# Handing over each MLP group's result one to three steps later, with one pool of four PSUM banks, in an attention and gated-MLP kernel

## The chip, the cores and the metric

The kernel runs on one core of one Trainium2 chip. The metric is device time in microseconds (us), lower is better. A core has five engines that run their own instruction streams in order and wait for each other on semaphores: TensorE (PE, with its weight loads shown as PEld), VectorE (DVE), ScalarE (ACT), GpSimd (POOL) and SyncE (SP), which here only issues DMA transfers. TensorE writes its products to PSUM, which has eight banks; each tile of this kernel's PSUM pools is one bank of 128 x 512 fp32.

## The reference, cut to what matters

Eight batches, eight heads, 576 positions, head width 64. Attention is masked by blocks of 64; its output, with the heads side by side (576 x 512), goes into a gated MLP whose gate mixes positions.

```python
scores = scale * np.matmul(q, k.transpose(0, 1, 3, 2))
scores = np.where(mask, scores, -1000000000.0)
attn = np.exp(scores - np.max(scores, axis=-1, keepdims=True))
attn = attn / (np.sum(attn, axis=-1, keepdims=True) + 1e-09)
x = np.matmul(attn, v)
...
h = np.maximum(x @ w_in, 0.0)
u, v = (h[..., :d_ff // 2], h[..., d_ff // 2:])
v_n = (v - mu) / np.sqrt(var + 1e-06)
v_s = np.einsum('ts,bsd->btd', w_spatial, v_n) + b_spatial[None, :, None]
out = (u * v_s) @ w_out
```

## The kernel before, in words

Operands are held as a high part and a remainder, so that most products are three matmuls: high by high, high by low, low by high. The work is cut into *steps*. A pair of heads of one batch takes NS = 7 steps, one for each slot of `SLOTS`: slots 0 and 1 are query tiles 0 and 1 of the two heads, 2 and 3 are query tile 2, 4 and 5 are query tile 3, and slot 6 is the last 64 queries of both heads. A batch has four pairs, so 28 steps.

For a pair (b, pr), by tile names in the profile:

- Scores `s`. `scores` (L261) issues slots 0 to 3 in step 0 and slots 4 and 5 in step 2, `scores_last` (L280) slot 6 as two banks in step 5. The two heads of a slot pair use different rows of the array, and the code issues their matmuls in turn. The banks come from `ps_s`, four of them.
- `exps` (L293) on DVE adds the mask and finds the maximum (L309, L318), which frees the score bank; ACT takes the exponential into tile `p` (L325).
- `norm` (L331): two small DVE instructions on the sums, then POOL scales `p` (L343).
- `transposes` (L384): DVE turns `p` into `q` in 32 x 32 blocks (L395, L400), and `move` issues 16 DMA transfers on SP that bring the blocks of `q` to their places in the single tile `turned` (L410). For batch 0 and the very last pair `transposes_pe` does it on TensorE instead.
- `av` (L431): the products of `turned` with `v` in two banks, `avl` and `avh` (L445, L462). `x_evac` (L423) takes the high part out on ACT and the remainder on DVE, into tile `x` (L426, L427).
- `prep_pair` (L222) splits the next pair's `raw` keys and queries into `hi` (ACT) and `lo` (DVE for the first 512 query columns, POOL for the rest, L232).

The MLP of batch b (`moe`, L477) is 29 *groups*, each one PSUM bank: five `mv` groups (gate half, positions in rows, with mean and variance taken over the row afterwards), eight `mu` groups (the other half), and then for each half z of the positions four `ms` groups (the mixing over positions) and four `mo` groups (output). A group's matmuls are followed at once, in the program's text, by all the work on its result: the `mv` group by evacuation (L499), statistics, normalization and splitting into `vh` and `vl` (L515 to L552); `mu` by L567; `ms` by the product with `u` on DVE (L592), the high part `gh` on ACT (L593) and the remainder `gl` on POOL, or on DVE for the fourth; `mo` by a copy on ACT (L612) and a DMA from ACT's queue. These groups are taken from a queue in the step loop at a little over one per step, beside the attention of the next batch. Their banks come from `ps_m`, two of them; transposes on TensorE and `av` have `ps_t`, two more.

The step loop (L677 to L735) sets the order in which the program is written. The instructions are then put in their final order, engine by engine, by a list scheduler that keeps to the written order as a priority and places an instruction earlier where its inputs and its tile's buffer are free. Each engine runs its own list in order.

Of the kernel before, what the change touches and what calls it, by code (L numbers as in the profile page):

```python
# [17 lines left out]
P = 128  # L18
# [16 lines left out]
RUN2, LAST, AV_AT, MOVES = 2, 5, 2 * NS + 1, 4  # L35
# [7 lines left out]
def kernel(  # L43
# [32 lines left out]
    ps_t = ctx.enter_context(tc.tile_pool(name="ps_t", bufs=2, space=PSUM))  # L76
    ps_m = ctx.enter_context(tc.tile_pool(name="ps_m", bufs=2, space=PSUM))
# [50 lines left out]
    def prep_w(hi, lo, w, rows, cols, name):  # L128
# [12 lines left out]
        f = ff_p.tile([P, 512], F32, tag="vr", name=f"f{name}", bufs=2)[:, :n]  # L141
# [63 lines left out]

    raws = {}
# [15 lines left out]
    def prep_pair(b, pr):  # L222
# [8 lines left out]
        for n, cs in enumerate((slice(S, Q8), slice(0, HT), slice(HT, S), slice(Q8, KQ))):  # L231
            (nc.vector if n == 0 else nc.gpsimd).tensor_tensor(  # L232
                out=lo[:, cs], in0=raw[:, cs], in1=hi[:, cs].bitcast(F32), op=ALU.subtract
            )
            yield
# [119 lines left out]
    def transposes_pe(b, pr, i):  # L355
# [3 lines left out]
        def bank(tag):  # L359
            return ps_t.tile([P, 512], F32, tag="t", name=f"t_{b}_{pr}_{tag}")  # L360
# [62 lines left out]
    def x_evac(b, pr, av, q0, n):  # L423
        x = x_tiles(b, pr)
        qs = slice(q0, q0 + n)
        nc.scalar.copy(x[:, 0, qs], av[:, :n])  # L426
        nc.vector.tensor_tensor(  # L427
            out=x[:, 1, qs], in0=av[:, :n], in1=x[:, 0, qs].bitcast(F32), op=ALU.subtract
        )

    def av(b, pr):  # L431
# [3 lines left out]
        al = ps_t.tile([P, 512], F32, tag="t", name=f"avl_{b}_{pr}")  # L435
        ah = ps_t.tile([P, 512], F32, tag="t", name=f"avh_{b}_{pr}")
# [22 lines left out]
        for c in range(5):  # L459
# [9 lines left out]
        x = xts[(b, pr)]  # L469

        nc.gpsimd.tensor_scalar(
            out=tails[b][:, pr], in0=x[:, :, FULL * P:].bitcast(F32), scalar1=1.0, scalar2=1.0,
            op0=ALU.mult, op1=ALU.mult,
        )


    def moe(b):  # L477
# [3 lines left out]
        u = ff_p.tile([P, ND, S], F32, tag="u", name=f"u_{b}")  # L481

        def v_group(c):
            ps = ps_m.tile([P, 512], F32, tag="m", name=f"mv_{b}_{c}")
            vr = ff_p.tile([P, DH], F32, tag="vr", name=f"vr_{b}_{c}", bufs=2)
# [3 lines left out]
            if c < FULL:  # L489
# [9 lines left out]
                nc.scalar.activation(vr, ps, AF.Relu)  # L499
            else:  # L500

                m = S - FULL * P
                for k in range(NC):
# [6 lines left out]
                nc.scalar.copy(vr[:m, :], ps[m:2 * m, :])  # L510
                nc.vector.tensor_tensor(out=vr[:m, :], in0=ps[:m, :], in1=vr[:m, :], op=ALU.add)
                nc.vector.tensor_scalar(
                    out=vr[:m, :], in0=vr[:m, :], scalar1=0.0, scalar2=None, op0=ALU.max
                )
            nc.vector.bn_stats(out=st[:m, 0:6], in_=vr[:m, :])  # L515
# [267 lines left out]
```

## Time and profile before

| | |
|---|---|
| runs of the kernel | 790.95, 791.2, 800.11 us; median 791.2 us |
| the profiled execution | 788.31 us, of which the span from first to last instruction is 786.5 us |
| mean granted TensorE clock | 0.961 |
| busy: DVE, ACT, POOL | 485.7, 424.9, 305.6 us |
| DMA | 92.05 MB, mean 117 GB/s |

A profile page has six parts: busy time of each engine; the span in 40 slices; DMA queues; the chain of work that ended last, followed back from the end; the costliest groups of instructions with the idle time of their engine before them; and DMA issues. Matmuls overlap each other, and their ends are modelled, so a busy share of PE is not its share of peak. Where a row of the timeline has a number in brackets, the engine stood idle that long before it, and the name behind the arrow is what ended the idle time. Line numbers are those of the code above.

### The profile page before, as it was taken

To read this page: it belongs to the slowest core of one execution; us is meant where nothing else is said; L and a number is where in the kernel's file an instruction comes from. 1 tells how busy PE (TensorE), PEld (TensorE's weight loads), DVE (VectorE), ACT (ScalarE), POOL (GpSimd) and SP (SyncE) were. 2 spreads that over 40 slices of the span, in tenths; PEclk is the share of its full clock that TensorE was granted. 3 is DMA by queue.
4 is the path that set the end of the run, shared out by engine and by line. 5 is a ranking of instruction groups with operands and counts; after the bars stand their busy time and mean duration, and the time that the engine had idled before them with its cause. 6 is when DMAs were issued, how large, how long until landed. Compare 5 with 4: busy or idle time off the path is not lost.

```text
span 786.5 us, 16421 instructions
## 1 busy us (share of the span) xinstructions
PE 719.0 (91%) x5729; PEld 621.8 (79%) x5729; DVE 485.7 (62%) x1639; ACT 424.9 (54%) x1148; POOL 305.6 (39%) x481
## 2 busy tenths in 40 slices
PE   8989689988999899998989979899798989999998
PEld 5656467877889788887779968798687877899898
DVE  6985797656766566547676465766576656731431
ACT  6876645545645465535664446555464446552542
POOL 4876446435154323334334441443224533231011
PEclk9989989997999999899999999999999999999999
DMA  6633344456345553255442453445613554333001
GB/s 208 197 115 90 105 122 131 105 141 172 88 120 155 157 135 76 74 154 151 130 123 72 134 163 95 131 110 146 185 46 108 155 158 103 82 89 89 1 8 54
DMA packets 42150, 92.05 MB, mean 117 GB/s; under 512 B 9298, under 2 KB 18002, under 8 KB 42068
## 3 DMA queue, kind: packets, MB, share of 16 engines
q1 hardware_dynamic: 32852, 81.56, 38.1%
q10 hardware_dynamic: 9216, 9.44, 3.5%
q8 instruction: 45, 0.74, 0.4%
q14 instruction: 37, 0.30, 0.1%
HBM read 38.18 MB, written 9.44 MB: 61 GB/s over the span
## 4 chain that ended last, share of the span: by engine, by line
PE 34%; DVE 21%; ACT 12%; POOL 7%; DMA 6%; issue 6%; SPq 3%; DVEq 0%; ACTq 0%; POOLq 0%
PE ms L585 12%; PE mo L606 11%; DVE q L395 6%; ACT p L325 4%; DMA raw<-qk 3%; DVE p L309 3%; POOL p L343 3%; POOL lo L232 3%; SPq L410 3%; ACT vr L535 3%; DVE st L515 2%; DVE vl L542 2%; PE s L274 2%; PE avl L445 2%; DMA outT<-o 2%
## 5 line engine op out<-in xcount | busy, mean ns | idle before, releaser
L325 ACT ACTIVATE p<-p,nmax 128x128 f32<-128x128 f32 (+4 forms) x288 | 166.9, 580 | 121.7 <-DVE nmax L309 92.4
L343 POOL TENSOR_SCALAR p<-p,ssum 128x128 f32<-128x128 f32 (+4 forms) x288 | 164.7, 588 | 170.7 <-DVE ssum L339 106.5
L395 DVE STREAM_TRANSPOSE q<-p 128x384 f32<-128x384 f32 (+1 forms) x189 | 113.6, 621 | 56.8 <-POOL p L343 31.9
L562 PE MATMUL mu<-x,wi_hi 128*128 128x288 f32 x512 | 117.9, 306 | 11.8 <-ACT u L567 3.4
L309 DVE CUSTOM_DVE_ANT_0 p<-s,mask 128x128 f32<-128x128 f32 (+3 forms) x256 | 116.0, 473 | 15.0 <-PE t L372 6.8
L232 POOL TENSOR_TENSOR lo<-raw,hi 128x288 fp32r<-128x288 f32 (+1 forms) x84 | 65.2, 798 | 142.1 <-ACT hi L229 142.1
L562 PEld LDWEIGHTS mu<-x,wi_hi 128*128 128x128 f32 x512 | 86.5, 190 | 25.2 <-DVE x L427 7.1
L494 PE MATMUL mv<-wi_hi,x 128*128 128x512 f32 x256 | 88.7, 408 | 0.0
L585 PE MATMUL ms<-ws_hi,vh 128*128 128x288 f32 x256 | 78.7, 307 | 8.1 <-ACT u L567 6.2
L585 PE MATMUL ms<-ws_lo,vh 128*128 128x288 f32 x256 | 77.0, 301 | 0.0
L585 PE MATMUL ms<-ws_hi,vl 128*128 128x288 f32 x256 | 77.0, 301 | 0.0
L592 DVE TENSOR_TENSOR u<-ms,u 128x288 f32<-128x288 f32 x64 | 29.0, 453 | 73.4 <-PE ms L590 73.1
L606 PE MATMUL mo<-gh,wo_hi 128*128 128x288 f32 x256 | 72.3, 304 | 1.1 <-DVE u L592 0.7
L606 PE MATMUL mo<-gh,wo_lo 128*128 128x288 f32 x256 | 71.9, 301 | 0.0
L562 PE MATMUL mu<-x,wi_lo 128*128 128x288 f32 x256 | 71.7, 300 | 0.0
L274 PE MATMUL s<-hi 64*128 64x128 f32 (+2 forms) x224 | 56.1, 384 | 11.2 <-DVE nmax L309 8.5
L594 POOL TENSOR_TENSOR gl<-u,gh 128x288 fp32r<-128x288 f32 x48 | 38.8, 809 | 70.7 <-ACT gh L593 70.1
L593 ACT CAST gh<-u 128x288 fp32r<-128x288 f32 x64 | 27.5, 430 | 71.2 <-DVE u L592 71.2
L585 PEld LDWEIGHTS ms<-ws_hi,vh 128*128 128x128 f32 x256 | 49.7, 194 | 13.8 <-ACT u L567 8.9
L494 PEld LDWEIGHTS mv<-wi_hi,x 128*128 128x128 f32 x256 | 49.1, 192 | 13.7 <-ACT o L612 1.8
L445 PE MATMUL avh<-turned,v 128*64 128x128 f32 x868 | 59.2, 293 | 0.0
L445 PEld LDWEIGHTS avh<-turned,v 128*64 128x64 f32 x868 | 54.7, 149 | 0.0
(122 smaller groups left out, 1600.8 us busy)
## 6 DMA issues: line engine op xcount, KB each, us to landing
turned<-q SPq DMA_DIRECT2D x216, 100.0 KB, 2.2
turned<-q SPq DMA_DIRECT2D x216, 96.0 KB, 2.2
raw<-qk SPq DMA_DIRECT2D x31, 608.0 KB, 4.1
v<-v SPq DMA_DIRECT2D x32, 320.0 KB, 3.3
outT<-o ACTq DMA_DIRECT2D x64, 144.0 KB, 2.0
rwi<-w_in SPq DMA_DIRECT2D x8, 512.0 KB, 4.9
rwo<-w_out SPq DMA_DIRECT2D x4, 512.0 KB, 4.7
rws<-w_spT SPq DMA_DIRECT2D x4, 288.0 KB, 3.4
```

Source lines behind the costliest of these rows:

```text
L232: (nc.vector if n == 0 else nc.gpsimd).tensor_tensor(out=lo[:, cs], in0=raw[:, cs], in1=hi[:, cs].bitcast(F32), op=ALU.subtract)
L274: nc.tensor.matmul(banks[(b, pr, i + hd)][:, o:o + n], a[js, qs], k[js, :n], start=(m == 0), stop=(m == len(parts) - 1),)
L309: nc.vector.tensor_tensor_reduce(out=pt[:, o:o + n], in0=bk[:, o:o + n], in1=mask[:, 512 - n:], scale=-0.125, scalar=BIG, op0=ALU.add, op1 ...
L325: nc.scalar.activation(pt[:, o:o + n], pt[:, o:o + n], AF.Exp, bias=mx, scale=-1.0, accum_out=ssum[:, s0 + r:s0 + r + 1],)
L343: nc.gpsimd.tensor_scalar(out=pt[:, o:o + w], in0=pt[:, o:o + w], scalar1=ssum[:, r:r + 1], scalar2=1.0, op0=ALU.mult, op1=ALU.mult,)
L395: nc.vector.transpose(to[:, :, o:o + 32 * n].rearrange("p r (c j) -> p c r j", j=32), pt[:, :n * P].rearrange("p (c r j) -> p c r j", r=4, ...
L445: nc.tensor.matmul(out[js, (t0 - q0) * P:(t1 + 1 - q0) * P].rearrange("p (t a j) -> p a t j", a=4, j=32), vt[:, c, js], src[:, :, o:o + 32 ...
L494: nc.tensor.matmul(ps, xs[k][:, j, cs], w[:, k, DH:], start=(n == 0), stop=(n == 3 * NC - 1),)
L562: nc.tensor.matmul(ps[:, :HT], w[:, k, ds], xs[k][:, j, zs], start=(n == 0), stop=(n == 3 * NC - 1),)
L585: nc.tensor.matmul(ps[:, :HT], a[:, ds], w[:, k, zs], start=(n == 0), stop=False)
L594: (nc.vector if dc == ND - 1 else nc.gpsimd).tensor_tensor(out=gl[:, dc, :], in0=uz, in1=gh[:, dc, :].bitcast(F32), op=ALU.subtract)
L606: nc.tensor.matmul(ps[:, :HT], w[:, k, es], a[:, k, :], start=(n == 0), stop=(n == 3 * ND - 1),)
```

## The change

Results are handed over later. A small agenda, `later(steps, phase, f)`, holds a piece of code until a step and one of four places in it; `due(phase)` runs what has come due.

```diff
+    def later(steps, phase, f):
+        todo.setdefault((now[0] + steps, phase), []).append(f)
+
+    def due(phase):
+        for f in todo.pop((now[0], phase), ()):
+            f()
```

One pool of four banks takes the place of two pools of two; `transposes_pe` and `av` take their banks from it too.

```diff
-    ps_t = ctx.enter_context(tc.tile_pool(name="ps_t", bufs=2, space=PSUM))
-    ps_m = ctx.enter_context(tc.tile_pool(name="ps_m", bufs=2, space=PSUM))
+    ps_m = ctx.enter_context(tc.tile_pool(name="ps_m", bufs=4, space=PSUM))
...
-        al = ps_t.tile([P, 512], F32, tag="t", name=f"avl_{b}_{pr}")
-        ah = ps_t.tile([P, 512], F32, tag="t", name=f"avh_{b}_{pr}")
+        al = ps_m.tile([P, 512], F32, tag="m", name=f"avl_{b}_{pr}")
+        ah = ps_m.tile([P, 512], F32, tag="m", name=f"avh_{b}_{pr}")
```

The work behind each group becomes closures. For `x` and the four kinds of group:

```diff
+        later(1, 0, hi)
+        later(1, 1, lo)
...
+            later(1, 0, evac)
+            later(1, 2, stats)
+            later(2, 1, scale)
+            later(2, 2, normal)
+            later(3, 1, rest)
...
+            later(0 if dc == ND - 1 else 1, 2 if dc == ND - 1 else 0, gate)
+            later(0 if dc == ND - 1 else 1, 2 if dc == ND - 1 else 1, split_g)
...
+            later(1, 0, leave)
```

An `ms` group now waits in the queue until all five `mv` results are complete, and an `mo` group until its four `gh` and `gl` are; the credit for groups is capped at two; the `mo` group takes its matmuls k by k, the three products of a k together:

```diff
-            for a, ws in ((gh, (wo_hi, wo_lo)), (gl, (wo_hi,))):
-                for k in range(ND):
-                    for w in ws:
+            for k in range(ND):
+                for a, w in ((gh, wo_hi), (gh, wo_lo), (gl, wo_hi)):
...
-        credit += rate
-        while credit >= 1.0 and queue:
-            queue.pop(0)()
+        credit = min(credit + rate, 2.0)
+        while credit >= 1.0 and queue and queue[0][0]():
+            queue.pop(0)[1]()
```

From batch 1 on, slots 0 and 1 are issued in step 0, slots 2 and 3 in step 1; `av` moves from step 15 to step 16 after its pair's start, and a batch's groups enter the queue one step after its last `av`:

```diff
-        if here and i == 0:
-            scores(*here, (0, 1, 2, 3))
...
+        if here:
+            if i == 0:
+                scores(*here, (0, 1, 2, 3) if boot else (0, 1))
+            elif i == 1 and not boot:
+                scores(*here, (2, 3))
+            elif i == 2:
+                scores(*here, (4, 5))
...
-RUN2, LAST, AV_AT, MOVES = 2, 5, 2 * NS + 1, 4
+LAST, AV_AT, BOOT_AV, MOVES = 5, 2 * NS + 2, NS + 2, 4
...
+                    later(1, 3, lambda b=pairs[of][0]: begin(b))
```

Work changes engine: all of `lo` goes to POOL (288 + 288 + 288 + 352 columns for each pair), the fourth `gl` too, and `vs_b`, a copy of 64 x 512 once in a batch, from DVE to ACT.

```diff
-        for n, cs in enumerate((slice(S, Q8), slice(0, HT), slice(HT, S), slice(Q8, KQ))):
-            (nc.vector if n == 0 else nc.gpsimd).tensor_tensor(
+        for cs in (slice(S, S + HT), slice(0, HT), slice(HT, S), slice(S + HT, KQ)):
+            nc.gpsimd.tensor_tensor(
...
-            (nc.vector if dc == ND - 1 else nc.gpsimd).tensor_tensor(
...
+                nc.gpsimd.tensor_tensor(
```

The rows `vr` have three buffers instead of two, and the preparation of the weights in batch 0 and 1 is spread a few steps later.

Three places of the order in which the instructions now stand, with buffer numbers behind the names (`s_6_0_1` is the score bank of batch 6, pair 0, slot 1). First TensorE at the start of pair (6, 0). Before:

```order
L274 MATMUL s_6_0_0_6580<-hi_6_0_6345 128x128
L274 MATMUL s_6_0_1_6581<-hi_6_0_6345 128x128
L274 MATMUL s_6_0_0_6580<-lo_6_0_6346,hi_6_0_6345 128x128
L274 MATMUL s_6_0_1_6581<-lo_6_0_6346,hi_6_0_6345 128x128
L274 MATMUL s_6_0_0_6580<-hi_6_0_6345,lo_6_0_6346 128x128
L274 MATMUL s_6_0_1_6581<-hi_6_0_6345,lo_6_0_6346 128x128
L274 MATMUL s_6_0_0_6580<-hi_6_0_6345 128x256
L274 MATMUL s_6_0_1_6581<-hi_6_0_6345 128x256
```

TensorE at the same place, after:

```order
L297 MATMUL s_5_3_6_1_6479<-hi_5_3_6051,lo_5_3_6052 128x288
L285 MATMUL s_6_0_0_6547<-hi_6_0_6355 128x128
L285 MATMUL s_6_0_0_6547<-lo_6_0_6356,hi_6_0_6355 128x128
L285 MATMUL s_6_0_0_6547<-hi_6_0_6355,lo_6_0_6356 128x128
L285 MATMUL s_6_0_0_6547<-hi_6_0_6355 128x256
L285 MATMUL s_6_0_0_6547<-lo_6_0_6356,hi_6_0_6355 128x256
L285 MATMUL s_6_0_0_6547<-hi_6_0_6355,lo_6_0_6356 128x256
L464 MATMUL avl_5_1_6358<-turned_122,v_5_1_6106 64x4x2x32 x2
L464 MATMUL avl_5_1_6358<-turned_122,v_5_1_6106 64x128 x2
L464 MATMUL avh_5_1_6359<-turned_122,v_5_1_6106 64x128 x14
L481 MATMUL avh_5_1_6359<-turned_122,v_5_1_6106 64x64 x10
L606 MATMUL mu_4_1_3_6392<-x_4_0_4916,wi_hi_110 128x288
```

Slot 0 now stands alone, right behind the previous pair's last scores and ahead of `av`; slot 1 follows five groups later (`mu_4_1_3`, then the four `ms_4_0`). Over the whole program, of the matmuls of slots 0 and 1 from batch 1 on, 61 of 168 with 128 columns and 60 of 168 with 256 stand away from their sibling head before, and 150 and 119 after; of slots 2 to 5, 25 of 336 before and 5 after.

Second TensorE at the head of batch 4's MLP. Before:

```order
L274 MATMUL s_5_2_0_6004<-hi_5_2_5727,lo_5_2_5728 128x256
L445 MATMUL avl_4_3_5736<-turned_125,v_4_3_5503 64x4x2x32 x2
L445 MATMUL avl_4_3_5736<-turned_125,v_4_3_5503 64x128 x2
L445 MATMUL avh_4_3_5737<-turned_125,v_4_3_5503 64x128 x14
L462 MATMUL avh_4_3_5737<-turned_125,v_4_3_5503 64x64 x10
L494 MATMUL mv_4_0_5834<-wi_hi_113,x_4_3_5766 128x512
L494 MATMUL mv_4_0_5834<-wi_lo_114,x_4_3_5766 128x512
```

TensorE at the same place, after:

```order
L285 MATMUL s_5_2_0_5946<-hi_5_2_5735,lo_5_2_5736 128x256
L464 MATMUL avl_4_3_5738<-turned_122,v_4_3_5498 64x4x2x32 x2
L464 MATMUL avl_4_3_5738<-turned_122,v_4_3_5498 64x128 x2
L464 MATMUL avh_4_3_5739<-turned_122,v_4_3_5498 64x128 x14
L481 MATMUL avh_4_3_5739<-turned_122,v_4_3_5498 64x64 x10
L665 MATMUL mo_3_1_1_5772<-gh_3_1_5581,wo_hi_112 128x288
L665 MATMUL mo_3_1_1_5772<-gh_3_1_5581,wo_lo_113 128x288
L665 MATMUL mo_3_1_1_5772<-gl_3_1_5582,wo_hi_112 128x288
```

Before, the product that needs `x_4_3` comes directly behind the `av` that makes it; after, three whole `mo` groups of batch 3 stand between. Between two `av` there now stand 8, 7, 7 and 7 groups in each of the batches 1 to 5; before, counted by their matmuls, 8.6, 8.8, 8.7 and 2.9, the last of these just ahead of the `av` shown. Behind the very last `av` stand 39 groups, where there were 28.

Third DVE around the `ms` groups of the first half of batch 4. Before:

```order
L592 TENSOR_TENSOR u_4_5804<-ms_4_0_0_6392,u_4_5804 128x288
L309 ISA p_5_3_4_6495,nmax_5_3_4_6493<-s_5_3_4_6431,mask_96 128x512
L309 ISA nmax_5_3_4_6493 128x1
L592 TENSOR_TENSOR u_4_5804<-ms_4_0_1_6439,u_4_5804 128x288
L592 TENSOR_TENSOR u_4_5804<-ms_4_0_2_6467,u_4_5804 128x288
L592 TENSOR_TENSOR u_4_5804<-ms_4_0_3_6502,u_4_5804 128x288
L594 TENSOR_TENSOR gl_4_0_6391<-u_4_5804,gh_4_0_6390 128x288
L395 STREAM_TRANSPOSE q_5_3_6485<-p_5_3_0_6321 128x3x4x32
```

DVE, after:

```order
L406 STREAM_TRANSPOSE q_5_3_6439<-p_5_3_4_6445 128x4x4x32
L347 TENSOR_SCALAR ssum_5_3_6_6516<-ssum_5_3_6_6516 128x1
L443 TENSOR_TENSOR x_5_1_6407<-avl_5_1_6358,x_5_1_6407 128x256
L443 TENSOR_TENSOR x_5_1_6407<-avh_5_1_6359,x_5_1_6407 128x320
L350 RECIPROCAL ssum_5_3_6_6516<-ssum_5_3_6_6516 128x1
L406 STREAM_TRANSPOSE q_5_3_6439<-p_5_3_5_6487 128x4x4x32
L639 TENSOR_TENSOR u_4_5909<-ms_4_0_0_6423,u_4_5909 128x288
L406 STREAM_TRANSPOSE q_5_3_6439<-p_5_3_6_6517 128x4x4x32
L411 STREAM_TRANSPOSE q_5_3_6439<-p_5_3_6_6517 128x2x32
L639 TENSOR_TENSOR u_4_5909<-ms_4_0_1_6462,u_4_5909 128x288
```

The products of the `ms` groups have moved behind the previous pair's transposes and behind the two evacuations of `av`; the fourth `gl` has left DVE.

More of the change, by code (lines that the diff above doesn't have):

```diff
@@ L735 @@
                     moving.append(move(b, pr))
-    for q in queue:
-        q()
+        due(3)
 def words(a):
```

249 lines of the change are left out of this document (144 added, 105 removed).

## The prediction

> **What bounds the kernel now.** I read the page first, for the span and the chain of work that ended last, then the windows, cut at the `av` of pair 1 of each batch.
>
> ```profile
> span 786.5 us, 16421 instructions
> ...
> PE 34%; DVE 21%; ACT 12%; POOL 7%; DMA 6%; issue 6%; SPq 3%; DVEq 0%; ACTq 0%; POOLq 0%
> ```
>
> ```profile
> 0.00:67.30 67.30, 57.59 (x392) 37.54 (x392) 50.75 (x171) 48.42 (x134) 44.06 (x65) 0.92 0.50 161
> 67.30:143.20 75.90, 63.81 (x455) 53.31 (x454) 57.41 (x179) 43.91 (x116) 38.47 (x53) 0.93 0.41 112
> 143.20:235.40 92.20, 83.50 (x686) 72.62 (x685) 60.43 (x205) 50.25 (x137) 38.32 (x61) 0.94 0.48 129
> 235.40:329.10 93.70, 88.05 (x701) 77.77 (x702) 58.68 (x204) 50.05 (x137) 35.11 (x58) 0.93 0.45 123
> 329.10:422.60 93.50, 86.56 (x706) 76.03 (x708) 59.08 (x204) 49.89 (x137) 35.52 (x58) 0.96 0.45 124
> 422.60:515.40 92.80, 85.34 (x706) 74.99 (x708) 59.06 (x204) 49.78 (x137) 35.52 (x58) 0.98 0.45 124
> 515.40:607.90 92.50, 85.05 (x707) 74.74 (x708) 58.99 (x204) 50.12 (x137) 35.55 (x58) 0.98 0.46 125
> 607.90:697.90 90.00, 84.54 (x704) 74.89 (x700) 56.46 (x199) 48.82 (x135) 32.83 (x56) 0.98 0.43 114
> 697.90:786.50 88.60, 84.59 (x689) 79.88 (x688) 24.81 (x69) 33.69 (x78) 10.24 (x15) 1.00 0.17 50
> ```
>
> After the window and its length the columns are busy time of PE, PEld, DVE, ACT and POOL, then the granted clock. From 143 us on a batch takes 90 to 94 us, and only PE is near its limit: DVE is busy 59 of 93 us. The chain passes through every engine, so it is no single engine that sets the end but PE plus what it waits for. What a steady batch could give back is PE's idle time plus what the lower clock took (one minus the granted clock, times the window). For the six windows from 143.2 to 697.9 that is 8.7 + 5.5, 5.7 + 6.6, 6.9 + 3.7, 7.5 + 1.9, 7.5 + 1.9 and 5.5 + 1.8, together 63 us. For 67.3 to 143.2 it is 12.1 + 5.3 = 17 us. The last window, with MLP work alone, stands at clock 1.00.
>
> The waits of PE in one steady batch (who waited, for whom, total, times, longest):
>
> ```profile
> PE avl L445 <- DMA turned<-q: 3.1, 1, 3.1
> PE s L274 <- DVE nmax L309: 1.3, 1, 1.3
> PE mu L562 <- DVE x L427: 1.3, 1, 1.3
> PE ms L585 <- ACT u L567: 1.0, 1, 1.0
> ```
>
> Four single waits, each at one place of the order: `av` comes too soon after the last one for the transfers between; slots 0 to 3 ask for four score banks at once; `mu` wants the newest `x`; `ms` wants the bank of a `mu` not yet evacuated. In the window from 67.3 us on the two-bank pool shows the same fault:
>
> ```profile
> PE mv L505 <- ACT vr L499: 4.6, 1, 4.6
> PE mu L562 <- ACT u L567: 2.6, 2, 2.2
> ```
>
> **The change, part by part.** *The wait of `av`.* The transfers of `turned` may start only when the last `av` has read it.
>
> ```profile
> 448.87 11.53 SPq L410 DMA_DIRECT2D turned<-q  x16
> ```
>
> ```profile
> 458.16 0.32 PE L274 MATMUL s<-hi 64*128 64x128 f32 x1
> ...
> 458.84 0.28 PE L274 MATMUL s<-hi,lo 64*128 64x256 f32 x1
> 462.19 0.87 PE L445 MATMUL avl<-turned,v 128*64 128x256 f32 x8 [3.07 <-DMA turned<-q]
> ```
>
> ```profile
> 515.33 0.87 PE L445 MATMUL avl<-turned,v 128*64 128x256 f32 x8
> ...
> 518.24 0.40 PE L606 MATMUL mo<-gh,wo_lo 128*128 128x288 f32 x1
> ...
> 519.37 0.33 PE L274 MATMUL s<-hi 64*128 64x128 f32 x2
> ...
> 520.16 0.34 PE L274 MATMUL s<-hi 64*128 64x384 f32 x2
> ```
>
> ```profile
> 506.55 0.40 PE L585 MATMUL ms<-ws_hi,vh 128*128 128x288 f32 x1 [0.99 <-ACT u L567]
> 506.79 0.30 PE L585 MATMUL ms<-ws_lo,vh 128*128 128x288 f32 x1
> 506.92 0.30 PE L585 MATMUL ms<-ws_hi,vl 128*128 128x288 f32 x1
> ```
>
> Sixteen issues take SP 11.53 us, the last lands 1.8 us later (460.40 to 462.19), and the `av` itself takes 2.9 us (515.33 to 518.24): 16.2 us from `av` to `av` at least. The new order has at least 7 groups between two. Matmuls start 0.13 us apart (506.79, 506.92), so a group of 12 is 1.6 us or more, and 7 groups, the scores (some 4 us, an estimate from the 0.79 us that slots 0 and 1 take together, 519.37 to 520.16) and the `av` are 18 us. The wait of 3.1 us goes, with about 2 us to spare.
>
> *The newest `x`.* Three `mo` groups (4.8 us) now stand behind `av`, and the evacuations fit beside them: the wait of 1.3 us goes. *Four banks.* A group may find its bank occupied only when the fourth group back is not evacuated, 6 us earlier; that covers the waits for `u` and `vr`. Every new late step on ACT or DVE is covered by that distance; without it, one such wait costs the 1.0 us of its row.
>
> *What is late next.* Two of the four banks are held by `avl` and `avh`, so the third group behind an `av` waits for DVE's `x` instruction. Here the durations are from the same steady batch:
>
> ```profile
> L232 POOL TENSOR_TENSOR lo<-raw,hi 128x288 fp32r<-128x288 f32 x8 | 6.7, 864 | 22.1 <-ACT hi L229 22.1
> ```
>
> ```profile
> L395 DVE STREAM_TRANSPOSE q<-p 128x384 f32<-128x384 f32 x16 | 8.4, 555 | 5.1 <-DMA turned<-q 5.1
> L395 DVE STREAM_TRANSPOSE q<-p 128x512 f32<-128x512 f32 x12 | 8.4, 707 | 4.4 <-POOL p L343 4.4
> L309 DVE CUSTOM_DVE_ANT_0 p<-s,mask 128x512 f32<-128x512 f32 x8 | 5.3, 662 | 0.0
> L232 DVE TENSOR_TENSOR lo<-raw,hi 128x512 fp32r<-128x512 f32 x4 | 2.7, 685 | 0.2 <-ACT hi L229 0.2
> ```
>
> Between slots 4 and 5 being ready and the `x` of `avl`, DVE now has four transposes of 0.56, one of 0.71, two maxima of 0.66, four shorter ones (at most 0.66 each) and small sums: 7 to 8 us. PE meanwhile has slot 6 and slot 0 (1.6), `av` (2.9) and two groups (3.2 to 3.5): about 8 us. That is a near tie. I allow 0.6 us of new waiting for each of 27 pairs, 16 us in all; the bounds are 0 (DVE ahead) and 3.6 us a pair (POOL's whole new `lo`, 1,216 columns at 0.864 us for 288, in front of the scaling that a transpose waits for). I stay near the lower end because that scaling is ahead of the last piece in POOL's order.
>
> *Work that changes engine.* POOL's `lo` grows from 704 to 1,216 columns, at 0.864 us for 288 a growth of 1.5 us for each pair, and DVE loses 0.685 us. POOL is busy 36 of 93 us, so this lies beside other work, unless it delays a scaling as just bounded. The fourth `gl` on POOL ends perhaps 0.4 us later than on DVE; in the tail, where no scores stand between, that may show twice: +1 us. The `vs_b` copy and the k-by-k order of `mo` issue the same matmuls and cost nothing that PE sees.
>
> *Scores apart.* Slot 0 alone takes 458.16 to about 459.0, 0.84 us for one head; together the two heads take 519.37 to 520.16, 0.79 us. So a head that stands alone adds about 0.42 us for six matmuls, near 0.06 for one of 128 columns and 0.08 for one of 256. 89 more of the first and 59 more of the second stand alone: +10 us; 20 of the wide ones join again: -2 us. I take +8 us; the bounds are 0 and 12.
>
> *The clock.* The wait of 506.55, one batch earlier:
>
> ```profile
> 412.32 0.61 PE L585 MATMUL ms<-ws_hi,vh 128*128 128x288 f32 x1 [0.99 <-ACT u L567]
> 412.73 0.44 PE L585 MATMUL ms<-ws_lo,vh 128*128 128x288 f32 x1
> ```
>
> The same 0.99 us wait is followed by matmuls of 0.44 us here and of 0.30 us at 506.79, so a short wait may or may not cost clock. [...] By the row, the clock can go on costing up to the 1.9 us a batch of the steady windows, 11 us in six.
>
> *Start.* From 0 to 67 us PE is not the limit; transposes, `av` and slots 4 and 5 of batch 0 now share one pool in written order. I take 0, with -5 and +8 as bounds. From 67.3 to 143.2 I take back the two bank waits, 7 of the 17 us, since DVE is busy there 57 of 76 us with the weights.
>
> The sum against the profiled execution of 788.3 us: 63 less 16 comes back in the steady batches (-47), 7 at the start, +8 for scores apart, +1 in the tail: 743. The median of the runs, 791.2, lies 2.9 us above that execution, so I say 746 us.
>
> **The rivals.** *Clean:* DVE stays ahead at the two banks, and all 63 and 17 us come back: 788 - 80 + 9 + 3 = 720 us. For it speaks that no engine but PE is over 65% busy; against it the near tie. *Half:* the in-order chain through DVE and ACT ends last in most pairs, 21% and 12% of the chain now; 30 us come back, none at the start: 788 - 30 + 9 + 3 = 770 us. *No change:* the change does not do what it says: every wait removed returns at the next bank (0 of 80 us back), and only half of the 21 us of clock is saved: 788 - 10 + 9 + 3 = 790 us. For it speaks that the chain passes through all engines; against it that the four waits shown have four different places, all moved apart. *Slower:* POOL decides. The `lo` pieces stand in its queue between the scalings of slots 3 and 6, a transpose of DVE waits for the scaling, the `x` of `avl` stands behind that transpose, and PE's third group behind `x`: 3.6 us for each of 27 pairs, 97 us. Without new waits the sum would be 788 - 63 - 7 + 9 + 3 = 730 us, with them 827 us. It ends over 2% slower, above 807 us, from 2.9 us a pair on. Against it speak POOL's 57 idle us a batch. [...]
>
> **How the numbers follow.** Forecast (728 to 760 us) 0.48, clean (below 728) 0.17, half (760 to 775) 0.16, no change 0.13, slower 0.06. A measurement here tells 2%, 16 us, from no change, so faster means below 775: 0.81; within 2%: 0.13; slower: 0.06. The range from 714 to 778 reaches into clean and half and leaves about 2 in 10 out, at both ends; the bounds of the clock (11 us) and 0.6 us of waits a pair either way (16 us) lie inside.
>
> **What would show it.** Right: PE's wait for `turned` and for `x` gone in the steady batches, a batch of 84 to 88 us from `av` to `av`, granted clock near 0.99 there, slots 0 and 1 of one pair in separate rows. The new waits, if any, should be of a third or fourth group for `x`, with POOL's scaling behind it. Wrong: batches of 92 us or more, or a first window far over 67 us.

## The result and the profile after

| | median us | range |
|---|---|---|
| before, 4 runs | 792.6 | 790.95 to 800.11 |
| changed, 4 runs | 763.8 | 762.24 to 765.95 |

The ratio is 0.962, with a 95% interval of 0.955 to 0.969: faster, by 29 us. The prediction said 746 us. The profiled execution took 762.2 us.

The page of the changed kernel, with the span, the busy times and the chain of work that ended last:

```profile
span 760.4 us, 16376 instructions
...
PE 717.2 (94%) x5729; PEld 621.4 (82%) x5729; DVE 459.7 (60%) x1587; ACT 425.8 (56%) x1156; POOL 339.4 (45%) x525
...
PE 50%; DVE 16%; ACT 15%; POOL 10%; issue 6%; DMA 1%; SPq 0%; POOLq 0%; DVEq 0%; ACTq 0%
```

PE is now half of the chain (34% before), and DMA, 6% before, is almost out of it. The windows of the changed kernel, cut at the same places as in the prediction (the `av` of pair 3 of batch 0, which is also what the prediction's first cut is, and from batch 1 on the `av` of pair 1 of each batch); after the length stand the busy times of PE, PEld, DVE, ACT and POOL, then the granted clock:

```profile
0.00:62.40 62.40, 51.41 (x384) 33.97 (x384) 48.35 (x167) 47.01 (x132) 44.61 (x65) 0.95 0.49 164
62.40:134.20 71.80, 58.16 (x396) 48.74 (x394) 53.06 (x174) 44.85 (x118) 44.23 (x59) 0.85 0.47 131
134.20:221.80 87.60, 84.03 (x667) 72.53 (x666) 53.32 (x190) 46.75 (x130) 37.39 (x61) 0.97 0.48 132
221.80:309.90 88.10, 87.02 (x705) 76.22 (x704) 55.58 (x198) 50.36 (x140) 39.53 (x64) 0.98 0.47 131
309.90:397.80 87.90, 85.42 (x705) 74.94 (x704) 55.69 (x198) 50.10 (x139) 39.86 (x65) 1.00 0.48 131
397.80:485.70 87.90, 85.45 (x705) 74.91 (x704) 55.72 (x198) 50.13 (x139) 39.84 (x65) 1.00 0.48 131
485.70:573.60 87.90, 85.42 (x705) 74.92 (x704) 56.39 (x198) 50.12 (x139) 39.87 (x65) 1.00 0.48 131
573.60:659.60 86.00, 84.16 (x699) 74.04 (x698) 55.62 (x197) 48.60 (x136) 36.10 (x60) 1.00 0.45 120
659.60:760.40 100.80, 96.12 (x774) 91.15 (x773) 26.00 (x72) 37.90 (x91) 17.92 (x27) 1.00 0.15 44
```

Two things are to be read here. A steady batch takes 87.9 us, and PE is idle for only 2.5 us of it at full clock. The second window, though, has PE idle for 13.6 us and the clock at 0.85, worse than the 12.1 us and 0.93 of the second window before, although fewer matmuls stand in it (396 rows against 455). The tail window is 12 us longer because more MLP groups stand in it (774 rows against 689); PE is busy 95% of it.

The waits of PE in one steady batch (397.8 to 485.7 us): who waited, for whom, total, times, longest:

```profile
PE ms L630 <- DVE x L443: 1.7, 1, 1.7
PE s L285 <- DVE nmax L320: 0.4, 2, 0.2
PE s L297 <- DVE nmax L320: 0.4, 1, 0.4
```

The four waits of before are gone, `turned` among them. What is left is the wait that the prediction allowed for: the third group behind an `av` waits for DVE's `x`, since `avl` and `avh` hold two of the four banks. It comes once a batch. The timeline of PE around it:

```profile
404.15 0.29 PE L635 MATMUL ms<-ws_b,vs_b 97*128 97x288 f32 x1
406.10 0.40 PE L630 MATMUL ms<-ws_hi,vh 128*128 128x288 f32 x1 [1.66 <-DVE x L443]
406.34 0.30 PE L630 MATMUL ms<-ws_lo,vh 128*128 128x288 f32 x1
```

The second matmul behind the wait takes 0.30 us again, and the granted clock from 406.1 to 409 us is 1.00: this wait costs no clock. Slot 0 of a later pair stands alone in front of an `av`, its rows x1, one head:

```profile
396.95 0.32 PE L285 MATMUL s<-hi 64*128 64x128 f32 x1 [0.22 <-DVE nmax L320]
...
397.62 0.28 PE L285 MATMUL s<-hi,lo 64*128 64x256 f32 x1
397.83 0.87 PE L464 MATMUL avl<-turned,v 128*64 128x256 f32 x8
```

Six matmuls of one head take 0.88 us (396.95 to 397.83).

The waits of PE at the start, from 62.4 to 134.2 us, and the timeline of POOL, DVE and PE around the longest of them:

```profile
PE s L285 <- DVE nmax L329: 6.1, 2, 5.5
PE s L297 <- DVE nmax L320: 4.5, 3, 2.0
PE s L285 <- DVE nmax L320: 2.3, 2, 1.4
```

```profile
93.70 4.63 POOL L243 TENSOR_TENSOR lo<-raw,hi 128x288 fp32r<-128x288 f32 x4 [3.49 <-ACT hi L240]
98.29 1.26 POOL L124 TENSOR_TENSOR wo_lo<-fwo,wo_hi 128x512 fp32r<-128x512 f32 x1
```

```profile
99.58 0.43 DVE L145 TENSOR_SCALAR fwo<-rwo 128x512 f32<-128x512 f32 x1 [1.95 <-POOL wo_lo L124]
...
101.95 0.50 DVE L329 CUSTOM_DVE_ANT_0 p<-s,mask,nmax 128x288 f32<-128x288 f32 x1
```

```profile
102.51 0.69 PE L285 MATMUL s<-hi 64*128 64x384 f32 x1 [5.50 <-DVE nmax L329]
```

Read upwards: PE waits 5.50 us for a score bank, which DVE's maximum at 101.95 frees. That maximum stands in DVE's list behind a weight conversion (99.58), which waits for a buffer that POOL's `wo_lo` has read, and this stands in POOL's list behind four pieces of `lo`, 4.63 us, all POOL's since the change.

### The profile page after: what moved, and what is told of

It reads as the page before. It is cut to its first block, busy times and chain, and to the rows that moved or that the text cites. A ratio compares the mean times of both kernels' runs of the same rounds, so it can differ in the third digit from the quotient of the medians.

```text
span 760.4 us, 16376 instructions
## 1 busy us (share of the span) xinstructions
PE 717.2 (94%) x5729; PEld 621.4 (82%) x5729; DVE 459.7 (60%) x1587; ACT 425.8 (56%) x1156; POOL 339.4 (45%) x525
## 4 chain that ended last, share of the span: by engine, by line
PE 50%; DVE 16%; ACT 15%; POOL 10%; issue 6%; DMA 1%; SPq 0%; POOLq 0%; DVEq 0%; ACTq 0%
PE mo L665 13%; PE ms L630 11%; PE s L285 7%; ACT p L336 5%; POOL lo L243 4%; PE avh L464 4%; POOL p L354 4%; PE mv L512 4%; PE mu L606 3%; ACT vr L566 3%; DVE p L320 3%; DVE st L542 3%; DVE q L406 2%; PE avl L464 2%; PE s L297 2%
## 5 line engine op out<-in xcount | busy, mean ns | idle before, releaser
L354 POOL TENSOR_SCALAR p<-p,ssum 128x128 f32<-128x128 f32 (+4 forms) x288 | 159.0, 567 | 206.4 <-DVE ssum L350 100.1
L243 POOL TENSOR_TENSOR lo<-raw,hi 128x288 fp32r<-128x288 f32 x112 | 94.3, 865 | 90.4 <-ACT hi L240 90.4
L649 POOL TENSOR_TENSOR gl<-u,gh 128x288 fp32r<-128x288 f32 x64 | 51.4, 806 | 91.4 <-ACT gh L648 91.3
L512 PE MATMUL mv<-wi_hi,x 128*128 128x512 f32 x256 | 85.3, 395 | 0.0
L665 PE MATMUL mo<-gh,wo_hi 128*128 128x288 f32 x256 | 79.2, 309 | 0.0
L665 PE MATMUL mo<-gl,wo_hi 128*128 128x288 f32 x256 | 77.0, 301 | 1.7 <-POOL gl L649 1.4
L648 ACT CAST gh<-u 128x288 fp32r<-128x288 f32 x64 | 27.5, 433 | 87.9 <-DVE u L639 82.5
L285 PE MATMUL s<-hi 64*128 64x128 f32 (+1 forms) x224 | 64.5, 404 | 12.6 <-DVE nmax L329 6.1
L665 PE MATMUL mo<-gh,wo_lo 128*128 128x288 f32 x256 | 75.6, 295 | 0.0
L285 PEld LDWEIGHTS s<-hi 64*128 64x128 f32 x224 | 31.7, 188 | 35.5 <-issue 14.3
L464 PE MATMUL avh<-turned,v 128*64 128x128 f32 x868 | 56.7, 285 | 0.0
```

What stands on the lines that cost most here:

```text
L243: nc.gpsimd.tensor_tensor(out=lo[:, cs], in0=raw[:, cs], in1=hi[:, cs].bitcast(F32), op=ALU.subtract)
L285: nc.tensor.matmul(banks[(b, pr, i + hd)][:, o:o + n], a[js, qs], k[js, :n], start=(m == 0), stop=(m == len(parts) - 1),)
L354: nc.gpsimd.tensor_scalar(out=pt[:, o:o + w], in0=pt[:, o:o + w], scalar1=ssum[:, r:r + 1], scalar2=1.0, op0=ALU.mult, op1=ALU.mult,)
L464: nc.tensor.matmul(out[js, (t0 - q0) * P:(t1 + 1 - q0) * P].rearrange("p (t a j) -> p a t j", a=4, j=32), vt[:, c, js], src[:, :, o:o + 32 ...
L512: nc.tensor.matmul(ps, xs[k][:, j, cs], w[:, k, DH:], start=(n == 0), stop=(n == 3 * NC - 1),)
L649: nc.gpsimd.tensor_tensor(out=gl[:, dc, :], in0=uz, in1=gh[:, dc, :].bitcast(F32), op=ALU.subtract)
```

## The experiments

Each run but one is the changed kernel with one edit, or the best version so far with one more; the exception is the kernel before with one edit. Medians are of fresh runs, beside fresh runs of the kernel before on the same chip (its medians there: 793.6, 792.2, 793.3 and 793.8 us).

### Joint score tiles

```diff
-    ps_s = ctx.enter_context(tc.tile_pool(name="ps_s", bufs=4, space=PSUM))
+    ps_s = ctx.enter_context(tc.tile_pool(name="ps_s", bufs=2, space=PSUM))
...
+                two = ps_s.tile([P, 2, 512], F32, tag="s", name=f"s_{b}_{pr}_{i}")
+                for hd in range(2):
+                    banks[(b, pr, i + hd)] = two[:, hd]
```

> The changed kernel, but the score tiles of the two heads of a pair are halves of one tile of two banks, so that both come free together and slots 0 and 1 are issued in turn again. Theory A (the steady batches fell short because slots 0 and 1 stand apart: PE's score matmuls take 2.8 us a batch more after the change than before): about 2.5 us a batch less in seven batches, 744 to 750 us, PE busy time lower by some 15 us. Theory B (the price of the prediction, 8 us in all): 754 to 758 us. Rival (a pair of banks waits for the later of two heads, so PE's waits for nmax grow by what the matmuls save): 762 us or more, with waits for nmax of over 2 us a batch.

Measured: 752.3 us, ratio 0.949 (0.945 to 0.953). The window of a steady batch and its waits:

```profile
394.70:480.10 85.40, 81.82 (x707) 72.02 (x706) 56.64 (x197) 49.71 (x139) 40.59 (x65) 1.00 0.49 135
```

```profile
PE ms L636 <- ACT u L621: 1.3, 1, 1.3
PE s L290 <- DVE nmax L326: 1.1, 1, 1.1
PE s L303 <- DVE nmax L326: 1.0, 1, 1.0
```

```profile
408.28 0.33 PE L290 MATMUL s<-hi 64*128 64x128 f32 x2
...
408.96 0.28 PE L290 MATMUL s<-hi,lo 64*128 64x256 f32 x2
409.16 0.40 PE L671 MATMUL mo<-gh,wo_hi 128*128 128x288 f32 x1
```

Two heads now take the same 0.88 us (408.28 to 409.16) that one took alone. For four pairs that is 3.5 us a batch; PE is busy 81.82 us in a batch, 3.6 less than the 85.45 of before the edit, and 1.1 us of that goes into new waits. A batch is 2.5 us shorter, as Theory A has it, but the whole gains 11.5 us, not 14 to 20, and lies between the two theories: the start gives some back. The second window ends 4.4 us earlier, but the third (129.8 to 224.3) is 7 us longer, 94.5 us, with 4.2 us of waits of `mo` for `gh` and 3.9 us of the scores for `nmax`. The price of a lone head is settled; how much of it the change brought is reckoned below.

### No delay

```diff
     def later(steps, phase, f):
-        todo.setdefault((now[0] + steps, phase), []).append(f)
+        if phase < 3:
+            f()
+        else:
+            todo.setdefault((now[0] + steps, phase), []).append(f)
```

> The changed kernel, but what evacuates a group, an av or a spatial product is handed over at once, not one to three steps later; only the start of a new batch of MLP groups keeps its delay. Theory A (the order on PE, three groups behind av, and the four banks removed the waits; the delay only changes the order in the queues of ACT, DVE and POOL): 760 to 768 us. Rival (the delay carries the gain, because without it ACT and DVE stand waiting for a group in front of work that PE needs): 775 to 790 us, with PE's waits for x, u or nmax of 3 us a batch or more.

Measured: 768.5 us, 0.969 (0.965 to 0.974), just above the range of Theory A. The delay itself, the part of the change that gives it its name, is worth some 5 of the 29 us. In the batch from 401.2 us PE has a single group of waits, for DVE:

```profile
PE s L288 <- DVE nmax L323: 2.2, 2, 2.0
```

### Two pools, one pool, three banks

The first of these is the changed kernel with the two pools of before, the second the kernel before with nothing changed but one pool of four for the two of two, the third the changed kernel with three banks in the shared pool.

```diff
-    ps_m = ctx.enter_context(tc.tile_pool(name="ps_m", bufs=4, space=PSUM))
+    ps_t = ctx.enter_context(tc.tile_pool(name="ps_t", bufs=2, space=PSUM))
+    ps_m = ctx.enter_context(tc.tile_pool(name="ps_m", bufs=2, space=PSUM))
...
-        al = ps_m.tile([P, 512], F32, tag="m", name=f"avl_{b}_{pr}")
+        al = ps_t.tile([P, 512], F32, tag="t", name=f"avl_{b}_{pr}")
```

> The changed kernel, but with the two pools of before: two banks for transposes and av, two for the MLP groups. Theory A (four shared banks removed the waits for banks: 1.0 us a batch and its clock, 7 us at the start): 775 to 788 us, with PE's waits of mv, mu and ms for ACT or DVE back at 2 us a batch or more. Rival (the spacing of av and the finer steps did it; the banks are worth little, and fewer of the slots 0 and 1 stand apart, 90 instead of 150 matmuls of 128 columns): 757 to 766 us.

```diff
-    ps_t = ctx.enter_context(tc.tile_pool(name="ps_t", bufs=2, space=PSUM))
-    ps_m = ctx.enter_context(tc.tile_pool(name="ps_m", bufs=2, space=PSUM))
+    ps_m = ctx.enter_context(tc.tile_pool(name="ps_m", bufs=4, space=PSUM))
```

> The kernel before, with one edit: its two pools of two banks are one pool of four. Theory A (a shared pool hands out its banks in the order in which the code is written, so that av and groups keep that order: 7 or 8 groups between two av, as in the changed kernel, instead of 10, 10, 10 and 4): most of the gain comes with the pool alone, and what is left to the changed kernel is DVE's lo (7 us by the run with lo on DVE) and the delay (5 us by the run without it): 772 to 780 us, PE's wait for turned gone. Rival (the pool is worth only the waits for banks, 1.0 us a batch and some 7 us at the start; the rest came from where the code is written): 780 to 788 us.

```diff
-    ps_m = ctx.enter_context(tc.tile_pool(name="ps_m", bufs=4, space=PSUM))
+    ps_m = ctx.enter_context(tc.tile_pool(name="ps_m", bufs=3, space=PSUM))
```

> The changed kernel with three shared banks instead of four, one bank left unused. The order of groups and av on PE stays 7 or 8 between two av. Theory A (it is the order that the shared pool sets, not the number of banks): 764 to 772 us. Rival (the number of banks: with avl and avh in two of three, the second group behind each av waits for x, 1 to 3 us for each of 27 pairs, and every group waits for the evacuation of the one three before it): 790 us or more.

| | median us | ratio to before | groups between the four `av` of a batch |
|---|---|---|---|
| before | 792.6 | 1 | 10, 10, 10, 4 |
| changed, two pools | 818.3 | 1.032 (1.027 to 1.037) | 10, 9, 11, 4 |
| before, one pool of four | 771.5 | 0.972 (0.964 to 0.980) | 8, 7, 7, 7 |
| changed, three banks | 802.1 | 1.009 (1.006 to 1.013) | 8, 7, 7, 7 |
| changed | 763.8 | 0.962 (0.955 to 0.969) | 8, 7, 7, 7 |

The last column is counted in PE's list of instructions; a group that an `av` cuts in two counts on both sides. It shows the mechanism: with pools of their own, groups and `av` pass each other freely, and the scheduler packs them unevenly. A shared pool hands out banks in the written order, so in the steady batches seven or eight groups stand between any two `av` in all three rows with a shared pool. With two pools the wait for `turned` comes back, here in a steady batch (433.4 to 531.9 us), and the kernel is slower than before the change, which neither theory of that run had:

```profile
PE avl L465 <- DMA turned<-q: 3.8, 1, 3.8
```

The pool alone, put into the kernel before, brings 20.7 us by the medians (792.2 to 771.5, just under the range of Theory A; its four runs lie at 767.3, 767.8, 775.1 and 776.7 us) and takes that wait away. It has a price at the start, seen in its windows:

```profile
0.00:38.80 38.80, 31.85 (x176) 20.39 (x176) 25.84 (x93) 23.67 (x69) 19.25 (x33) 0.87 0.50 171
38.80:141.00 102.20, 81.80 (x619) 65.80 (x617) 81.34 (x255) 67.80 (x181) 63.48 (x86) 0.88 0.44 127
```

Up to 141 us PE's idle time (6.95 + 20.40) and the clock's share (5.0 + 12.3) are 44.7 us together, where the kernel before lost 32.5 us up to its same place (15.1 + 17.4 in the prediction's rows). This trace is of the run of 776.7 us, 9 us above the fastest of the four, so its clock's share may be high; the idle time alone is 27.4 us against 21.8. The number of banks counts too: with three, the order is the same and the rival's 790 us come true. In the batch from 420.5 to 512.6 us:

```profile
420.50:512.60 92.10, 87.61 (x705) 76.50 (x704) 55.80 (x198) 50.09 (x139) 39.74 (x65) 0.98 0.46 125
```

```profile
PE ms L630 <- DVE x L443: 3.2, 2, 2.6
```

So it is both: order first, and then four banks to be able to afford it. My Theory A of the three-bank run, order alone, fell.

### Lo on DVE

```diff
-        for cs in (slice(S, S + HT), slice(0, HT), slice(HT, S), slice(S + HT, KQ)):
-            nc.gpsimd.tensor_tensor(
+        for n, cs in enumerate((slice(S, Q8), slice(0, HT), slice(HT, S), slice(Q8, KQ))):
+            (nc.vector if n == 0 else nc.gpsimd).tensor_tensor(
```

> The changed kernel, but the first 512 columns of a pair's lo are DVE's again, as before the change. Theory A (at the start four lo pieces on POOL, 4.6 us, stand in front of a weight split and this in front of DVE's score work, a stall of PE of 5.5 us at 102 us at half clock): the stretch from 62 to 134 us is 4 to 8 us shorter, the steady batches unchanged, 756 to 760 us. Rival 1 (the later weight preparation, not POOL, makes that stall): 762 to 766 us. Rival 2 (POOL also limits the steady batches, as in the prediction's slower case): steady batches shorter by 1 us or more as well, below 754 us.

Measured: 771.1 us, 0.973 (0.968 to 0.979), slower than the changed kernel, which no theory had.

```profile
32.50:130.00 97.50, 79.64 (x606) 63.40 (x604) 81.22 (x255) 69.07 (x182) 64.42 (x87) 0.89 0.45 134
308.00:399.60 91.60, 88.06 (x707) 77.39 (x706) 59.31 (x201) 50.33 (x138) 36.60 (x60) 0.97 0.46 126
```

```profile
PE s L285 <- DVE nmax L320: 2.9, 2, 2.7
```

The start came out as Theory A says: `av` of pair 1 of batch 1 begins at 130.0 us, not 134.2. But a steady batch takes 90 to 92 us instead of 87.9: DVE's 0.7 us a pair come back as a wait of PE for `nmax` (the second fence is the batch from 399.6 us), and the clock stands at 0.97 in place of 1.00. DVE, busy 59 of 92 us, is late where PE needs it. No theory of mine had put a price on DVE's part.

### Score sets and av's step as before

```diff
-                scores(*here, (0, 1, 2, 3) if boot else (0, 1))
-            elif i == 1 and not boot:
-                scores(*here, (2, 3))
+                scores(*here, (0, 1, 2, 3))
```

> The changed kernel, but slots 0 to 3 are written together at step 0, as before. Theory A (the finer sets remove the wait for nmax of 1.3 us a batch with its clock, as the prediction has it): 770 to 776 us. Rival (the order on PE is set by when the score banks come free, not by the step at which the scores are written, and slots 0 and 1 stand apart all the same): 761 to 767 us.

```diff
-LAST, AV_AT, BOOT_AV, MOVES = 5, 2 * NS + 2, NS + 2, 4
+LAST, AV_AT, BOOT_AV, MOVES = 5, 2 * NS + 1, NS + 2, 4
```

> The changed kernel, but av is written at step 15 of its pair, as before, not 16. Theory A (the shared pool, not the step, keeps 7 or 8 groups between two av, so that av finds turned landed all the same): 761 to 767 us, no wait for turned in the steady batches. Rival (the later step is what lets the 16 transfers land): the wait for turned of 3 us a batch returns, 775 us or more.

Measured: 782.2 us, 0.984 (0.976 to 0.991), with runs from 773.1 to 785.8 us, and 785.1 us, 0.990 (0.986 to 0.994), with runs from 782.8 to 786.3 us. By the medians that is 18 and 21 us slower than the changed kernel, though groups stand between the `av` just as before the edit. The first time lies above what Theory A gives, the second where the rival puts it, and in neither run is the wait there that was to bring it. With the score sets, PE's waits in a batch are for `x` (2.2 us) and `gl` (0.9 us), and 0.3 us for `nmax`. The rival of the score sets is right on the order, not on the time: in the trace 156 of the 168 matmuls of 128 columns start over 30 ns away from the other head's, as against 150 in the changed kernel. Two batches in a row, then PE around the wait for `gl` in the first and in the second:

```profile
314.40:402.70 88.30, 84.50 (x707) 74.64 (x706) 55.25 (x197) 50.20 (x139) 40.30 (x65) 1.00 0.49 130
402.70:495.60 92.90, 89.04 (x705) 78.47 (x704) 55.58 (x197) 50.37 (x139) 40.24 (x65) 0.94 0.46 124
```

```profile
355.31 0.40 PE L665 MATMUL mo<-gl,wo_hi 128*128 128x288 f32 x1 [0.89 <-POOL gl L649]
355.64 0.50 PE L285 MATMUL s<-lo,hi 64*128 64x512 f32 x2
355.98 0.40 PE L285 MATMUL s<-hi,lo 64*128 64x512 f32 x2
...
445.15 0.40 PE L665 MATMUL mo<-gl,wo_hi 128*128 128x288 f32 x1 [0.89 <-POOL gl L649]
445.49 0.67 PE L285 MATMUL s<-lo,hi 64*128 64x512 f32 x2
445.95 0.63 PE L285 MATMUL s<-hi,lo 64*128 64x512 f32 x2
```

PE is idle for 3.8 and 3.9 us of them; the second is 4.6 us longer because its clock was 0.94. The same two pairs of score matmuls take 0.50 and 0.40 us behind the wait in the first batch, and 0.67 and 0.63 us behind the same wait in the second. With `av` a step earlier, no wait for `turned` is left, and one of 1.7 us for `nmax` stands in each batch:

```profile
407.60:499.50 91.90, 89.28 (x707) 78.95 (x706) 56.91 (x198) 50.02 (x138) 40.00 (x66) 0.95 0.46 125
```

```profile
493.72 1.35 PE L285 MATMUL s<-hi 64*128 64x512 f32 x2 [1.73 <-DVE nmax L320]
...
495.85 0.61 PE L297 MATMUL s<-hi 128*128 128x288 f32 x1
```

The row of 1.35 us holds two matmuls that start 0.55 us apart; the clock shows in the last row, 0.61 us where the same matmul takes 0.40 at full clock (356.30 us in the run with the score sets). PE is idle for 2.6 us, as in the changed kernel (2.5), but the clock falls behind that wait and the batch is 4 us longer. So the finer sets and the later `av` are worth 18 and 21 us by the medians, but not by the waits that were expected. Of the 18.8 and 20.6 us by which the two profiled spans are longer than that of the changed kernel, PE's idle time has 7.2 and 5.5 us; the rest, 11.6 and 15.1 us, is PE busy for longer, with 48 and 38 us more at half clock.

### The start

Three tries, all with joint score tiles. The first gives the first 512 columns of `lo` back to DVE, for batch 1 alone. The second prepares the weights at the steps of before. The third adds to the first a faster pace for batch 0's groups.

```diff
+        early = b == 1
...
+        for n, cs in enumerate(first if early else rest):
+            (nc.vector if early and n == 0 else nc.gpsimd).tensor_tensor(
```

> The kernel with joint score tiles, and the first 512 columns of lo are DVE's for the pairs of batch 1 alone, which are split before 134 us. Theory A (at the start POOL is the late one, in the steady batches DVE): the start is 3 to 5 us shorter and the steady batches stay at 85.4 us: 746 to 750 us. Rival (with joint tiles the start waits for DVE's weight conversions and maxima, not for POOL, so more work on DVE makes it longer): 752 to 757 us.

Measured: 749.2 us, 0.944 (0.938 to 0.950), the time of Theory A. The `av` of pair 1 of batch 2 begins at 220.6 us instead of 224.3, and the steady batches keep 85.4 us. The windows do not show the theory's reason, though: the one in which these pieces of `lo` stand (32.2 to 131.8 us) is 4.1 us longer than with joint tiles alone, while the one ahead of it is 2.1 us shorter and the one behind it 5.7. Where the gain comes from stays open. This is the best version of the study: 14.6 us under the changed kernel by the medians of two sittings.

```diff
-    spread(chain([prep_w_in(c, 0) for c in range(NC)]), 7 * NC + 1, U0 - 7, U0 + 6)
+    spread(chain([prep_w_in(c, 0) for c in range(NC)]), 7 * NC + 1, U0 - 7, U0 + 4)
...
-    spread(chain([prep_w_out(c) for c in range(ND)]), 7 * ND + 1, U0 + 10, U0 + 17)
+    spread(chain([prep_w_out(c) for c in range(ND)]), 7 * ND + 1, U0 + 8, U0 + 14)
```

> The kernel with joint score tiles, and the weights are prepared at the steps of before (two to three steps earlier). Theory A (the later preparation is why the start gained nothing: w_out's conversion stands between DVE's score work of batch 1, and the first mo waits for gh): 744 to 749 us, with 4 to 8 us less up to the av of pair 1 of batch 2. Rival (earlier conversions collide with the scores of batch 1 in DVE's queue, which is why they were moved): 752 to 760 us.

Measured: 752.2 us, 0.948 (0.942 to 0.955), the same as without it (752.3). One window gets longer (95.5 to 100.2 us) and the next as much shorter (94.5 to 89.3); with joint tiles, when the weights are prepared is not the cause.

```diff
-        steps = NPAIR * NS + (0 if b else AV_AT - BOOT_AV)
+        steps = NPAIR * NS
```

> The kernel with joint score tiles and the early lo on DVE, and batch 0's 29 MLP groups are spread over 28 steps, not 35, so that 12, 7, 7 and 3 of them stand between the av of batch 1, not 9, 6, 6 and 6. Theory A (the start loses time because the shared pool keeps the written order, and in it too few groups stand between the waits for DVE): PE's idle time up to the av of pair 1 of batch 2 falls by 3 to 8 us: 741 to 746 us. Rival (the waits for DVE's maxima follow each other whatever stands between them, or the early groups wait for weights that are not split yet): 748 to 756 us.

Measured: 768.4 us, 0.969 (0.967 to 0.971), a miss. PE's idle time and clock share up to the `av` of pair 1 of batch 1 fell from 43.9 us to 38.3, so groups do seem to fill waits there. The next window gave more back, and the steady batches lost 3 to 4 us each, and why stays open. The window of batch 1, a steady one, and the wait that is new in the first:

```profile
136.40:225.40 89.00, 74.16 (x627) 64.48 (x626) 53.31 (x190) 48.80 (x134) 37.90 (x61) 0.93 0.49 133
402.60:491.70 89.10, 85.42 (x705) 74.76 (x704) 56.97 (x197) 49.37 (x139) 40.04 (x65) 0.96 0.47 129
```

```profile
PE avl L473 <- DMA turned<-q: 8.2, 1, 8.2
```

The waiting `av` is that of pair 3 of batch 1, at 176.8 us, with only three groups ahead of it: PE reaches it 12.4 us after the `av` before (156.1 us), when the transfers, 16.2 us from `av` to `av` in the prediction's working, cannot be through.

### Vl on POOL

```diff
-                    nc.vector.tensor_tensor(
+                    nc.gpsimd.tensor_tensor(
                         out=vl, in0=vr, in1=vh.bitcast(F32), op=ALU.subtract
```

> The kernel with joint score tiles and the early lo on DVE, and the four vl subtractions of a batch (128x512 each) are POOL's, not DVE's. Theory A (DVE is the engine whose lateness PE still waits for in the steady batches, 2.1 us a batch for nmax, so that 2.8 us less on DVE shorten a batch by 0.5 to 2 us): 736 to 745 us. Rival (POOL's subtraction is later than DVE's and ms waits for vl, or DVE has enough room by now): 748 to 755 us.

Measured: 752.7 us, 0.950 (0.946 to 0.955): the rival, 3.5 us slower than without it. A steady batch is 85.2 to 85.4 us, as before the edit, and the third window 5 us longer. With joint tiles DVE has enough room in the steady batches.

## Why the prediction was right, and where it missed

The sign, the class and the range held (763.8 us in 714 to 778). The forecast of 746 us was 18 too low. The same reckoning as in the prediction, PE's idle time plus the clock's share, now from the rows after: six steady windows 18.3 us (63 before), the start 14.1 + 24.4 = 38.5 us (15.1 + 17.4 = 32.5 before), the tail 4.7 (4.0). These losses fell by 38 us and the span by only 26.1, so what PE does beyond them grew by the rest, 11.8 us.

| term | predicted | measured |
|---|---|---|
| steady batches | -47 | -44.7 |
| start | 0 and -7 | +6.0 |
| scores apart (measured: the rest) | +8 | +11.8 |
| tail | +1 | +0.7 |
| sum | -45 | -26.2 |

**Steady batches: right.** The four waits went, and the new one is the one named, the third group behind `av` for DVE's `x`. I allowed 0.6 us a pair, 2.4 us a batch; PE is idle 2.5 us. It is not spread over the pairs, though: 1.7 us come at one place of a batch. The reason given for `av`, seven groups between two, was right too, and the pool is what makes them seven, which the prediction did not say. I treated order and banks as two gains; the runs show that the shared pool makes the order (20.7 us alone) and that the order needs its four banks (38 us slower with three).

**The clock: right only for this one order.** I put its rest at 0, with 11 us as a bound, and the four last steady windows stand at 1.00. The runs with score sets and `av` as before show how near that was: PE idle for 3.8 and 2.6 us of a batch, not 2.5, and up to 5 us more in it. That the rest came out at 0 is in part luck: no run shows that an order with such waits is free of half clock. What the runs showed in its place is a mean clock of 0.97 to 1.00 in the six steady windows of the changed kernel, of 0.94 to 1.00 with the score sets and of 0.95 to 0.97 with `av`'s step as before.

**The start: this is the step that failed.** "From 67.3 to 143.2 I take back the two bank waits, 7 of the 17 us" and 0 before that. The two bank waits did go, but 13 us are missing against this term. The pool alone raises the loss up to that place from 32.5 to 44.7 us in its one trace, probably because in the written order fewer groups are at hand when PE waits for DVE (the faster pace for batch 0's groups took 43.9 to 38.3 there); and what the prediction costed at nothing, the longer `lo` on POOL, adds 4 us there (130.0 against 134.2 us). The later weight preparation, tried with joint tiles, does not. I had both facts before me, a start limited by engines other than PE and a pool in written order, and took the second for a gain alone. Why the changed kernel loses less at the start than the pool alone does (38.5 against 44.7 us) was not taken apart.

**Work that changes engine: costed at nothing, and not nothing on either engine.** "so this lies beside other work": at the start POOL's part does not, and in the steady batches DVE's relief is worth some 3 us each (90 to 92 us with `lo` on DVE). Together the move gains 7.3 us (771.1 to 763.8). The slower rival, POOL deciding in the steady batches, is refuted by the same run: with less on POOL they get longer. Nor did the moved pieces slow each other down: in a steady batch twelve `lo` pieces of 128x288 take POOL 805 ns each after the change, where eight took 864 ns before.

**Scores apart: right in kind and price.** A head that stands alone adds 0.44 us, half of the 0.88 us that one takes and two take as well; the prediction had 0.42. The 148 matmuls more that stand alone, a twelfth of 0.88 us each, are 10.9 us, less what rejoins. The 11.8 us of the table is no measurement of its own; with the clock from the trace's records in place of the two digits of the rows, the rest is 10.1 us. The heads come apart through the pool's order: in the trace of the kernel before with one pool 150 of the 168 matmuls of 128 columns stand alone too (62 before). It is a term that could be undone, by one tile for two heads.

**The rivals.** Clean did not come, because of the start and the scores. The time lies in the band of Half (760 to 775), but not by its mechanism: in the steady batches 45 of 63 us came back, and PE stands idle for only 2.5 of 87.9 us there. It lies above the band of the forecast itself (728 to 760).

## What to carry to other kernels

Under a scheduler like this one, a buffer pool shared by two kinds of work fixes their order as well as their number; ask of each pool what may pass what, and what then fills a wait. Cost work moved off an engine with a low busy share by the wait that ends behind it: DVE at 60% was worth 3 us a batch here. Two half-array matmuls that should run together are best kept together by giving them one tile, since a scheduler that sees two buffers may split them, as it did here (six score matmuls of one head alone took 0.88 us, those of two heads together the same).

## What the runs showed of the hardware

What a short wait of PE cost in clock differed from place to place in these traces. In the changed kernel a wait of 1.66 us between two `ms` groups left the clock at full speed (granted clock 1.00 from 402 to 408 us, 0.30 us a matmul behind the wait). One of 1.73 us between scores, in the run with `av` at step 15, was followed by slower matmuls (0.61 us for one that takes 0.40 at full clock, then 0.44 us each). The kernel before shows what clock goes with such rows: from 412.4 to 413.3 us its matmuls of 128x288 take 0.44 us, start 0.24 us apart, and the granted clock is 0.50; from 506.6 to 508 us they take 0.30 us, start 0.13 us apart, and it is 1.00.

Like waits did not cost alike. In the kernel before, the half clock just named stands behind the second of two waits, 1.30 us at 409.82 and 0.99 us at 412.32; one batch later, behind the second of a like pair, 1.29 us at 504.05 and 0.99 us at 506.55, again 2.50 us apart, the clock is full. With the score sets, PE is idle for 3.8 us of one batch, at a mean clock of 1.00 (88.3 us), and for 3.9 us of the next, at 0.94 (92.9 us). Over the whole spans the mean granted clock is 0.961 before, 0.975 after the change, 0.945 with the score sets and 0.952 with `av`'s step as before; that is PE at half clock for 61.4, 37.5, 85.3 and 75.1 us. What makes one wait fall on the clock and another not was not shown: no run here moves a wait and leaves the rest in place.
